# Attention and two expert layers on one core: q and k laid out by the host, another order of the first batch, a tighter conversion of the weights

## The chip, the cores and the metric

The kernel runs on one core of a Trainium2 chip. Its time is the device time of one execution in microseconds (us). The engines are TensorE (PE in the rows; PEld is its weight load), VectorE (DVE), ScalarE (ACT), GpSimd (POOL) and SyncE (SP), which here only issues DMAs. They work through their own queues in the order in which the program was written for each, and wait for one another by semaphores.

## What is computed

```python
# attention: q, k, v of 4 batches, 8 heads, 576 positions, 64 wide, float32
scores = (q @ k.T) / sqrt(64)
thresh = max(scores, axis=-1) - tau
scores = where(scores >= thresh, scores, -1e9)
attn = exp(scores - max(scores)); attn /= sum(attn) + 1e-9
x = (attn @ v)                       # as 2304 tokens x 512
# a feed-forward layer, w_in 512x2048 and w_out 2048x512, both float64
x = (relu(x @ w_in) ** 2) @ w_out
# slots: 8 experts with 4 slots each, hidden 1024
logits = x @ phi
d = softmax(logits, axis=0); c = softmax(logits, axis=1)
slots = d.T @ x
slot_out[e] = relu(slots[e] @ w1[e]) @ w2[e]      # e = 0 ... 7
out = c @ slot_out
```

## The kernel before

The work goes in pairs of heads, 16 in all, four to a batch. A pair has five query tiles: four of 128 queries of both heads from the first 512 positions (j = 0 to 3) and a mixed one (j = 4) with the last 64 queries of both heads. For each pair `prep` loads q, k and v. q and k come with positions on the partitions, and TensorE needs them with the head's width there, so `turn` transposes them by four 128x128 pieces each through the helper at L238, `evac` copies the result out of PSUM to `qt` and `kt` (L412), and `rturn`/`revac` do the same with the last 64 positions of both heads, loaded once a batch as `rem`, into a block diagonal tile `bd` whose other quarters are zero (L422).

`tiles` then makes, for each query tile: the scores (`s_mm`, L457 and L462, the mixed tile L451 and L454) into the one `s` buffer of PSUM; for each head on VectorE the scaled copy with its extreme (`top`, L478), on ScalarE the exponential (`expo`, L491), on VectorE the masked product with its sum (`keep`, L495); nine transposes of the result on TensorE and their copies on ScalarE (L534, L532). After each two tiles a group is closed: the sums' reciprocals, the product with v (L583, L572) and its scaling into `xp`, the input of the feed-forward part (L596). One unit of the feed-forward part is two query tiles of all four pairs of a batch, 256 tokens; there are eight and one for the remainders, nine in all (L867 is their first product). At most three `xp` tiles exist.

Beside the attention `conv_ops` turns the float64 weights into float32, in 32 chunks of 128x512: 16 of w_in (split into two float32r parts, L315 on ScalarE and L316 on GpSimd) and 16 of w_out (stored again by DMA, and multiplied with phi, L331). Each chunk has its load (L269, four buffers), a scale (L275), a low part (L285) and a shift (L289) on VectorE, and a sign, on GpSimd (L298) or on VectorE (L300). The first feed-forward product depends on all chunks.

The order of every queue is made when the program is written: `Plan` has each operation with an engine, a cost, what it depends on, the buffers it takes and a key. It runs a clock, and at each step gives each engine the ready operation with the smallest key. The keys are

```python
def key(p, x):
    return T0 + p * PC + x            # T0 = 20, PC = 20: a pair; TA = 4: a tile
k = C0 + n * TC                       # chunk n of the conversion: 2.604 + n * 3.458
```

to which LEAD adds a number for each kind of operation (c_scale 13.2, c_load -19.6, c_prod 65.3). Feed-forward products have keys from 100,000 on: they get TensorE when no attention is ready.

Of the kernel before, what the change touches and what calls it, by code (L numbers as in the profile page):

```python
# [9 lines left out]
F32 = mybir.dt.float32  # L10
# [4 lines left out]
AF = mybir.ActivationFunctionType  # L15
# [124 lines left out]
def tile_kernel(  # L140
# [11 lines left out]
    out: bass.AP,  # L152
):
    nc = tc.nc
    B, H, S, D = q.shape
    DM, DFF = w_in.shape
    NS = phi.shape[1]
    E, _, F = w1.shape
    NP = H // 2
# [9 lines left out]
    PAIRS = B * NP  # L169
# [3 lines left out]
    GB = 4  # L173
# [2 lines left out]
    PTB = 2  # L176
    XPB = 3
    MMB = 4
    RAWB = dict(q=1, k=1, v=2)
    WAIT = 0.0  # L180
    DQ = 2.212
    T0 = 20.0
    TA = 4.0
    PC = 20.0
    TC = 3.458
    C0 = 2.604
    LOWA = ()
    SGNP = (0, 2, 4, 6)
# [38 lines left out]
    l4 = const.tile([128, NU], F32, name="l4")  # L227
    dT = const.tile([NS, NU], F32, name="dT")
# [120 lines left out]
    def attn_ops():  # L349

        at, ac = state["at"], state["ac"]
        bd = [ac.tile([128, 2, 128], F32, name=f"bd{i}") for i in range(2)]
        vbd = [ac.tile([128, NP, 192], F32, name=f"vbd{i}") for i in range(2)]
        for t in bd + vbd:
            nc.gpsimd.memset(t, 0.0)
        ma, ps = psp["ma"], psp["s"]
        raw, rem = {}, {}
        P = [dict() for _ in range(PAIRS)]  # L360
        src = {"q": q, "k": k, "v": v}
        last = {}

        def key(p, x):
            return T0 + p * PC + x

        def prep(p):
            b, n, h0 = p // NP, p % NP, 2 * (p % NP)
            d = P[p]
            k0 = key(p - 1, 2.0) if p else 0.0  # L370
            ld = {}
            if n == 0:
                def lrem():
                    r = rem[b] = at.tile([128, NP, 2, D], F32, tag="qkrem", name="rem", bufs=1)
                    for a, nm in enumerate("qk"):
                        y = src[nm][b, :, 512:S, :].rearrange("(n h) p d -> p n h d", h=2)
                        nc.sync.dma_start(out=r[64 * a:64 * a + 64], in_=y)
# [5 lines left out]
                last["r"] = add("lrem", "SP", 1.3, lrem, [], k0 - 10, ["qkrem"], dma=0.74)  # L383
                last["v"] = add("lrem", "SP", 1.9, lvrem, [], k0 - 4, ["vbd"], dma=1.1)
            for nm in "qkv":
                def lraw(nm=nm):
                    if nm == "v":
                        t = raw[p, nm] = at.tile([128, 2, 4 * D], F32, tag=nm + "raw", name="raw", bufs=RAWB[nm])
# [10 lines left out]
            d["rem_op"], d["v_op"], d["vr_op"] = last["r"], ld["v"], last["v"]  # L399
            d["v"], d["vb"] = (lambda: raw[p, "v"]), vbd[b % 2][:, n, :]  # L400
            d["qbd"], d["kbd"] = bd[p % 2][:, 0, :], bd[p % 2][:, 1, :]

            o = {}

            def turn(nm):
                o[nm] = mm_tile()
                for j in range(4):
                    transpose(o[nm][:, j * 128:(j + 1) * 128], raw[p, nm][:, j].rearrange("p h d -> p (h d)"))

            def evac(nm):  # L410
                t = d[nm + "t"] = at.tile([128, 512], F32, tag=nm + "t", name=nm + "t", bufs=2)
                nc.scalar.activation(t, o[nm], AF.Copy)  # L412

            def rturn():
                o["r"] = mm_tile()
                transpose(o["r"][:, 0:128], rem[b][:, n].rearrange("p h d -> p (h d)"))

            def revac():
                y = o["r"][:, 0:128].rearrange("p (c s) -> p c s", c=2)
                for a in range(2):  # L420
                    i = slice(64 * a, 64 * a + 64)
                    nc.scalar.activation(bd[p % 2][i, :, i], y[i], AF.Copy)  # L422

            d["ready"] = []
            for i, nm in enumerate("kq"):
                t = add("qk_turn", "PE", 0.5, lambda nm=nm: turn(nm), [ld[nm]], k0 + 1 + i, ["mm", nm + "t"], [(nm + "raw", ld[nm])])
                e = add("qk_evac", "ACT", 0.6, lambda nm=nm: evac(nm), [t], k0 + 1 + i, [], [("mm", t)])
                d[nm + "_op"] = t
                d["ready"].append(e)
            t = add("qk_turn", "PE", 0.13, rturn, [d["rem_op"]], k0 + 3, ["mm", "bd"])  # L430
            e = add("qk_evac", "ACT", 0.55, revac, [t], k0 + 3, [], [("mm", t)])
            d["b_op"] = d["rt_op"] = t
            d["ready"].append(e)

        def tiles(p):
            d = P[p]
            b, kk = p // NP, p % NP
            G = [dict() for _ in range(3)]
            s_ops, av_ops, m_ops = [], [], []

            def tile_ops(n, j):
                k = key(p, n * TA)
                mixed = j == 4
                g = 2 if mixed else j // 2
                o, gd = {}, G[g]

                def s_mm():
                    s = ps.tile([128, 3, 512], F32, tag="s", name="s", bufs=1)
                    o["s"] = s.rearrange("p c s -> p (c s)")
                    if mixed:  # L450
                        nc.tensor.matmul(s[:, 0], d["qbd"], d["kt"], start=True, stop=True)  # L451
                        for a in range(2):
                            i = slice(64 * a, 64 * a + 64)
                            nc.tensor.matmul(s[i, 1, 0:64], d["qbd"][:, i], d["kbd"][:, i], start=True, stop=True)  # L454
# [173 lines left out]
                att.append(ev)  # L628
                av_ops.append(o)

            for n, j in enumerate(range(5)):
                tile_ops(n, j)
                if n % 2:
                    group_ops(n // 2, n)
                elif n == 4:
                    group_ops(2, n)
            for o in s_ops:
                plan.release(o, [("kt", d["k_op"]), ("qt", d["q_op"]), ("bd", d["b_op"])])
            for o in av_ops:
                plan.release(o, [("vraw", d["v_op"]), ("vbd", d["vr_op"])])  # L640
            plan.release(d["rt_op"], [("qkrem", d["rem_op"])])

        for p in range(PAIRS):
            prep(p)
            tiles(p)

    def small(shape, nm, bufs=2):
        return state["fs"].tile(shape, F32, tag=nm, name=nm, bufs=bufs)
# [523 lines left out]
```

## Time and profile before

| | |
|---|---|
| median of 3 runs | 756.98 us (754.79 to 757.75) |
| the profiled execution | 756.39 us |
| its span, first to last instruction | 754.6 us |
| TensorE busy | 691.3 us, 92% |
| VectorE busy | 422.9 us, 56% |
| ScalarE busy | 398.1 us, 53% |
| GpSimd busy | 133.8 us, 18% |
| mean granted clock of TensorE | 0.978 of full speed |

Busy times are shares of the whole span and average over stages that differ: conversion with attention, attention alone, attention with the feed-forward part, the feed-forward part alone, and the experts at the end. A matmul's listed duration includes its way through the array, and the next one starts before it ends; what one costs the engine is seen from the spacing of starts.

### The profile page before, as it was taken

What the parts mean: (1) busy time and instruction counts of PE and PEld (TensorE: products, weight loads), DVE (VectorE), ACT (ScalarE), POOL (GpSimd) and SP (SyncE); (2) the same over time, 40 slices, a digit from 0 to 9 for tenths busy, and PEclk for the clock granted to TensorE, in tenths of its full rate; (3) what the DMA queues carried; (4) which work ended last, traced back from release to release, by engine and by line L of the source; (5) the groups of instructions that cost most, each with busy time, mean ns of one, the idle gap of its engine ahead of it and who ended that gap; (6) DMA issues with size and microseconds to landing.
All of it is one profiled execution on the core that took longest, in us unless ns stands there. A gap on an engine that the chain in (4) does not pass through costs nothing.

```text
span 754.6 us, 13828 instructions
## 1 busy us (share of the span) xinstructions
PE 691.3 (92%) x5342; PEld 505.4 (67%) x5342; DVE 422.9 (56%) x1110; ACT 398.1 (53%) x790; POOL 133.8 (18%) x238
## 2 busy tenths in 40 slices
PE   1586998999999999999999999999999999998873
PEld 1253666677666686787567778767989889794311
DVE  6999888885667767625777462465133231403403
ACT  5667676777666666347667452564333343332203
POOL 5777221331121211100111100010000000000000
PEclk9978899999999999999999999999999999999998
DMA  8854545231111111010101000002920000197986
GB/s 238 229 151 150 161 140 199 86 109 43 45 27 46 36 29 45 1 43 29 29 23 23 1 1 1 29 3 90 400 84 29 1 29 2 32 357 282 388 322 251
DMA packets 70129, 78.81 MB, mean 104 GB/s; under 512 B 43952, under 2 KB 48048, under 8 KB 70064
## 3 DMA queue, kind: packets, MB, share of 16 engines
q1 hardware_dynamic: 70064, 77.94, 31.5%
q8 instruction: 42, 0.69, 0.4%
q14 instruction: 23, 0.19, 0.1%
HBM read 69.01 MB, written 8.91 MB: 103 GB/s over the span
## 4 chain that ended last, share of the span: by engine, by line
PE 79%; DVE 8%; DMA 4%; ACT 3%; issue 2%; SPq 1%; POOL 1%; POOLq 0%; DVEq 0%; ACTq 0%
PE mm L867 28%; PE mm L238 18%; PE po L583 9%; PE s L462 8%; PE mm L682 2%; PE mm L796 2%; PE po L572 2%; PE s L457 2%; DMA w<-in_moe_w_dram 2%; PE mm L998 2%; PE s L451 2%; DVE e L495 2%; DVE u L478 2%; DVE cv L289 2%; PE mm L331 1%
## 5 line engine op out<-in xcount | busy, mean ns | idle before, releaser
L867 PE MATMUL mm<-xh,w 128*128 128x256 f32 x1152 | 165.9, 287 | 0.0
L867 PEld LDWEIGHTS mm<-xh,w 128*128 128x128 f32 x1152 | 147.7, 191 | 13.7 <-issue 11.9
L495 DVE SCALAR_TENSOR_TENSOR e<-u,sm,e 128x576 f32<-128x576 f32 x144 | 120.8, 849 | 35.7 <-ACT e L491 34.0
L478 DVE TENSOR_SCALAR_CACHE_REDUCE u<-s,nscale 128x576 f32<-128x576 f32 x144 | 114.3, 811 | 44.4 <-PE s L462 39.3
L491 ACT ACTIVATE e<-u,sm 128x576 f32<-128x576 f32 x144 | 109.3, 777 | 26.0 <-DVE u L478 25.4
L534 ACT ACTIVATE pt<-mm 128x512 f32<-128x512 f32 x144 | 82.6, 596 | 56.0 <-PE mm L238 55.3
L873 ACT ACTIVATE gt<-mm 128x512 f32<-128x512 f32 x72 | 43.0, 597 | 122.8 <-PE mm L867 122.4
L238 PE MATMUL mm<-ident_r,e 128*128 128x128 f32 (+1 forms) x656 | 98.1, 285 | 9.5 <-DVE e L495 8.0
L484 POOL TENSOR_SCALAR sm<-sm,tau_p 128x1 f32<-128x1 f32 x144 | 53.6, 372 | 281.9 <-DVE u L478 218.7
L238 PEld LDWEIGHTS mm<-ident_r,e 128*128 128x128 f32 (+1 forms) x656 | 76.0, 144 | 38.2 <-issue 13.4
L867 PE MATMUL mm<-xl,w 128*128 128x256 f32 x576 | 92.4, 283 | 0.0
L867 PEld LDWEIGHTS mm<-xl,w 128*128 128x128 f32 x576 | 79.3, 192 | 0.0
L583 PE MATMUL po<-pt,raw 128*64 128x256 f32 (+1 forms) x768 | 78.3, 341 | 0.0
L462 PE MATMUL s<-kt,qt 64*128 64x512 f32 x256 | 75.1, 664 | 1.8 <-ACT kt L412 1.8
L583 PEld LDWEIGHTS po<-pt,raw 128*64 128x64 f32 x768 | 43.2, 139 | 28.6 <-issue 11.5
L879 DVE SCALAR_TENSOR_TENSOR gt<-mm,gt 128x512 f32<-128x512 f32 x18 | 12.4, 691 | 67.1 <-ACT gt L873 67.0
L238 PE MATMUL mm<-ident_r,gt 128*128 128x128 f32 x288 | 37.9, 277 | 0.1
L238 PEld LDWEIGHTS mm<-ident_r,gt 128*128 128x128 f32 x288 | 31.8, 143 | 9.2 <-issue 8.7
L881 ACT ACTIVATE gt<-gt 128x512 f32<-128x512 f32 x54 | 34.0, 630 | 1.5
L832 DVE CAST xh<-xp 128x256 fp32r<-128x256 f32 x32 | 10.5, 354 | 43.4 <-PE mm L867 43.3
L457 PE MATMUL s<-bd,qt 128*128 128x128 f32 x128 | 27.0, 293 | 7.9 <-DVE u L478 7.7
L838 POOL TENSOR_TENSOR xl<-xp,xh 128x256 fp32r<-128x256 f32 x16 | 11.6, 741 | 126.6 <-PE mm L867 126.2
(134 smaller groups left out, 828.6 us busy)
## 6 DMA issues: line engine op xcount, KB each, us to landing
w<-in_moe_w_dram SPq DMA_DIRECT2D x25, 1024.0 KB, 11.9
raw<-in_moe_w_in_dram SPq DMA_DIRECT2D x16, 512.0 KB, 4.6
raw<-in_moe_w_out_dram SPq DMA_DIRECT2D x16, 512.0 KB, 4.2
raw<-in_q_dram SPq DMA_DIRECT2D x32, 128.0 KB, 3.0
raw<-in_k_dram SPq DMA_DIRECT2D x32, 128.0 KB, 2.9
raw<-in_v_dram SPq DMA_DIRECT2D x16, 256.0 KB, 2.6
w_out<-cv SPq DMA_DIRECT2D x16, 256.0 KB, 3.7
w<-w_out SPq DMA_DIRECT2D x4, 1024.0 KB, 9.9
```

Source lines behind the costliest of these rows:

```text
L238: nc.tensor.transpose(out_, in_, ident[:n, :n])
L457: nc.tensor.matmul(s[:, 1].rearrange("p (c s) -> p c s", s=64)[:, 0:8:7], lt, d["kbd"], start=True, stop=True)
L462: nc.tensor.matmul(s[:, 2 * a], lt[i], d["kt"][i], start=True, stop=True)
L478: nc.vector.tensor_scalar(u, o["s"][:, s0:s0 + S], nscale, None, ALU.mult, ALU.min, accum_out=gd["sm"][:, c:c + 1])
L484: nc.gpsimd.tensor_scalar(sm[:, 4 + c:5 + c], sm[:, c:c + 1], tau_p, None, ALU.add)
L491: nc.scalar.activation(e, o["u", a], AF.Exp, scale=-1.0, bias=gd["sm"][:, c:c + 1])
L495: nc.vector.scalar_tensor_tensor(e, o["u", a], sm[:, 4 + c:5 + c], e, ALU.is_le, ALU.mult, accum_out=sm[:, 8 + c:9 + c])
L534: nc.scalar.activation(pt[:, 4 * x:4 * x + 4, i], o["p", x].rearrange("p (c s) -> p c s", c=4), AF.Copy)
L583: nc.tensor.matmul(po[i, :n_], lt, rh, start=m == 0, stop=m == 4)
L867: nc.tensor.matmul(o["h"][:, i * NU:(i + 1) * NU], a, c, start=n_ == 0, stop=n_ == len(terms) - 1)
L873: nc.scalar.activation(g, o["h"], AF.Relu)
L881: nc.scalar.activation(g, g, AF.Square)
```

## The change

The host hands over q and k already turned: for each batch and pair a tile of 128 rows (64 of each head) with 640 columns, 512 of the first positions in the order of the query tiles, then 128 in the block diagonal form with zeros. The kernel loads one such tile each for q and k into `qt` and `kt` (three buffers each) and multiplies from them; `turn`, `evac`, `rturn`, `revac`, `bd`, `rem` and their loads are gone. The pairs become 20 jobs: the four pairs of the first batch with query tiles 0 and 1, the same four with tiles 2 to 4, then the other twelve with all five; each job loads its own q, k and v. TC goes from 3.458 to 2.8.

```diff
-    RAWB = dict(q=1, k=1, v=2)
+    QKB = 3
-    TC = 3.458
+    TC = 2.8
-            gk=GB, l4=1, dT=1, qt=2, kt=2, bd=2, qraw=RAWB["q"], kraw=RAWB["k"], vraw=RAWB["v"], qkrem=1, vbd=2,
+            gk=GB, l4=1, dT=1, qt=QKB, kt=QKB, vraw=2, vbd=2,
...
+        jobs = [(p, js) for js in ((0, 1), (2, 3, 4)) for p in range(NP)]
+        jobs += [(p, (0, 1, 2, 3, 4)) for p in range(NP, PAIRS)]
+        P = [dict() for _ in jobs]
+        begins = [T0 + TA * sum(len(js) for _, js in jobs[:i]) for i in range(len(jobs))]
         def key(p, x):
-            return T0 + p * PC + x
+            return begins[p] + x
...
-                    t = raw[p, nm] = at.tile([128, 4, 2, D], F32, tag=nm + "raw", name="raw", bufs=RAWB[nm])
-                    for a in range(2):
-                        nc.sync.dma_start(
-                            out=t[:, :, a, :], in_=src[nm][b, h0 + a, 0:512, :].rearrange("(r j) d -> r j d", j=4)
-                        )
-                ld[nm] = add("lraw", "SP", 0.6 if nm == "v" else 1.2, lraw, [], k0 - (5 if nm != "v" else 2), [nm + "raw"], dma=0.73 if nm == "v" else 1.46)
+                    t = d[nm + "t"] = at.tile([128, SQ], F32, tag=nm + "t", name=nm + "t", bufs=QKB)
+                    nc.sync.dma_start(out=t, in_=src[nm][b, n])
+                ld[nm] = add("lraw", "SP", 0.6, lraw, [], k0 - (5 if nm != "v" else 2), [nm + ("raw" if nm == "v" else "t")],
+                             dma=0.73 if nm == "v" else 0.95)
...
-            for i, nm in enumerate("kq"):
-                t = add("qk_turn", "PE", 0.5, lambda nm=nm: turn(nm), [ld[nm]], k0 + 1 + i, ["mm", nm + "t"], [(nm + "raw", ld[nm])])
-                e = add("qk_evac", "ACT", 0.6, lambda nm=nm: evac(nm), [t], k0 + 1 + i, [], [("mm", t)])
...
-            t = add("qk_turn", "PE", 0.13, rturn, [d["rem_op"]], k0 + 3, ["mm", "bd"])
-            e = add("qk_evac", "ACT", 0.55, revac, [t], k0 + 3, [], [("mm", t)])
...
+            d["ready"] = [ld["q"], ld["k"]]
...
-                        s[:, 1].rearrange("p (c s) -> p c s", s=64)[:, 0:8:7], lt, d["kbd"], start=True, stop=True
+                        s[:, 1].rearrange("p (c s) -> p c s", s=64)[:, 0:8:7], lt, d["kt"][:, 512:SQ], start=True, stop=True
...
-                        nc.tensor.matmul(s[:, 2 * a], lt[i], d["kt"][i], start=True, stop=True)
+                        nc.tensor.matmul(s[:, 2 * a], lt[i], d["kt"][i, 0:512], start=True, stop=True)
...
-            for n, j in enumerate(range(5)):
+            for n, j in enumerate(jobs[p][1]):
...
+        if name in ("q", "k"):
+            m = a[:, :, :512].reshape(*a.shape[:2], 128, 4, -1).transpose(0, 1, 4, 3, 2).reshape(a.shape[0], -1, 128, 512)
+            r, z = a[:, :, 512:].transpose(0, 1, 3, 2), _np.zeros_like(a[:, ::2, 512:])
+            r = [_np.concatenate(x, axis=3) for x in ((r[:, ::2], z), (z, r[:, 1::2]))]
+            a = _np.concatenate([m, _np.concatenate(r, axis=2)], axis=3)
```

## Rows read from the trace of the kernel before

**Rows 1.** From the page: the span in 40 equal slices of 18.9 us. Digits are the busy share in tenths; GB/s is what the DMAs moved.

```profile
PE   1586998999999999999999999999999999998873
...
DVE  6999888885667767625777462465133231403403
...
GB/s 238 229 151 150 161 140 199 86 109 43 45 27 46 36 29 45 1 43 29 29 23 23 1 1 1 29 3 90 400 84 29 1 29 2 32 357 282 388 322 251
```

**Rows 2.** Busy time of each engine by stage: the stretch and its length in us, then busy us and count for PE, PEld, DVE, ACT and POOL, the mean granted clock of TensorE, the busy share of the DMA engines, GB/s.

```profile
0.00:83.00 83.00, 48.85 (x229) 30.17 (x229) 72.43 (x132) 53.95 (x100) 54.56 (x55) 0.86 0.65 193
83.00:157.00 74.00, 70.17 (x530) 49.22 (x526) 64.39 (x173) 54.23 (x108) 20.25 (x37) 1.00 0.45 142
157.00:180.20 23.20, 23.16 (x183) 16.70 (x182) 15.42 (x47) 16.52 (x36) 4.49 (x9) 1.00 0.21 59
180.20:686.00 505.80, 500.45 (x4051) 391.02 (x4049) 251.52 (x709) 261.06 (x525) 53.54 (x136) 1.00 0.18 60
```

**Rows 3.** The same view, of the first stretch without its first 10 us.

```profile
10.00:83.00 73.00, 48.85 (x229) 30.17 (x229) 67.53 (x120) 49.25 (x94) 49.85 (x44) 0.84 0.64 186
```

**Rows 4.** The instructions of two lines: L867, the first feed-forward product, and L275, the scale of a conversion chunk; durations in ns (least, median, most), then the first and last start in us.

```profile
L867 PE MATMUL mm<-xh,w x1152: 274/283/388, 180.2 to 675.9; 128*128 128x256 f32 x192
...
L275 ACT ACTIVATE cv<-raw x32: 647/674/714, 5.6 to 157.0; 128x512 f32<-128x512 f32 x32
```

**Rows 5.** Records of two score lines by stretch: PE busy us and count, PEld busy us and count, then the clock, the DMA share and GB/s as in rows 2. The first two rows are L457 (two records a tile), the last two L451 (two records a mixed tile).

```profile
0.00:83.00 83.00, 4.04 (x14) 2.90 (x14) 0.86 0.65 193
83.00:157.00 74.00, 5.02 (x24) 3.69 (x24) 1.00 0.45 142
...
0.00:83.00 83.00, 2.05 (x2) 0.50 (x2) 0.86 0.65 193
83.00:157.00 74.00, 3.23 (x6) 0.91 (x6) 1.00 0.45 142
```

**Rows 6.** TensorE in order of time, near 394 and 418 us: start, us, engine, line, operation, tiles, count. The rows with raw are q's and k's transposes, the one with rem is the remainders'.

```profile
393.35 0.60 PE L238 MATMUL mm<-ident_r,raw 128*128 128x128 f32 x4
393.79 0.60 PE L238 MATMUL mm<-ident_r,e 128*128 128x128 f32 x4
...
417.70 0.60 PE L238 MATMUL mm<-ident_r,raw 128*128 128x128 f32 x4
418.13 0.39 PE L457 MATMUL s<-bd,qt 128*128 128x128 f32 x2
...
419.51 0.66 PE L238 MATMUL mm<-ident_r,raw 128*128 128x128 f32 x4
420.00 0.27 PE L238 MATMUL mm<-ident_r,rem 128*128 128x128 f32 x1
```

**Rows 7.** The remainders' transposes on TensorE, one for each pair, by stretch: busy us and count (the count of the last row has one that reaches over the border).

```profile
0.00:83.00 83.00, 1.08 (x3) 0.86 0.65 193
83.00:180.20 97.20, 0.91 (x4) 1.00 0.39 122
180.20:686.00 505.80, 2.72 (x10) 1.00 0.18 60
```

**Rows 8.** TensorE in order of time from the start: its first transpose with what it waited for, and the first score matmuls.

```profile
11.65 0.66 PE L238 MATMUL mm<-ident_r,rem 128*128 128x128 f32 x2 [11.65 <-DMA rem<-in_k_dram]
...
17.02 0.77 PE L457 MATMUL s<-bd,qt 128*128 128x128 f32 x2
...
19.60 2.08 PE L462 MATMUL s<-kt,qt 64*128 64x512 f32 x4 [1.81 <-ACT kt L412]
```

**Rows 9.** VectorE's groups by line: operation, tiles, shapes, count, then busy us and the mean ns of one, and the idle time before them with what ended it.

```profile
L495 DVE SCALAR_TENSOR_TENSOR e<-u,sm,e 128x576 f32<-128x576 f32 x144 | 120.8, 849 | 35.7 <-ACT e L491 34.0 <-POOL rb L562 0.6 <-POOL sm L484 0.3
L478 DVE TENSOR_SCALAR_CACHE_REDUCE u<-s,nscale 128x576 f32<-128x576 f32 x144 | 114.3, 811 | 44.4 <-PE s L462 39.3 <-PE s L454 4.4
L289 DVE SCALAR_TENSOR_TENSOR cv<-cv,raw 128x512 int32<-128x512 int32 x32 | 30.4, 955 | 4.2 <-ACT cv L275 3.7
...
L285 DVE TENSOR_SCALAR raw<-raw 128x512 int32<-128x512 uint32 x32 | 17.7, 569 | 2.3 <-DMA raw<-in_moe_w_out_dram 1.5 <-DMA raw<-in_moe_w_in_dram 0.8
```

**Rows 10.** The conversion's two steps on VectorE with least, median and most ns, and three instructions in order of time, two of VectorE and one of GpSimd.

```profile
L285 DVE TENSOR_SCALAR raw<-raw x32: 399/422/1515, 5.6 to 147.2; 128x512 int32<-128x512 uint32 x32
...
L289 DVE SCALAR_TENSOR_TENSOR cv<-cv,raw x32: 672/688/1769, 6.3 to 158.2; 128x512 int32<-128x512 int32 x32
...
17.47 0.69 DVE L289 SCALAR_TENSOR_TENSOR cv<-cv,raw 128x512 int32<-128x512 int32 x1 [1.54 <-ACT cv L275]
...
19.27 1.47 POOL L298 TENSOR_TENSOR cv<-cv,raw 128x512 f32<-128x512 f32 x1
...
19.70 1.58 DVE L289 SCALAR_TENSOR_TENSOR cv<-cv,raw 128x512 int32<-128x512 int32 x1
```

**Rows 11.** What TensorE's transposes waited for in the first 90 us: total us, times, longest; here the one row for k's own load.

```profile
PE mm L238 <- DMA raw<-in_k_dram: 2.6, 1, 2.6
```

More of the change, by code (lines that the diff above doesn't have):

```diff
@@ L154, in tile_kernel @@
     nc = tc.nc
-    B, H, S, D = q.shape
+    B, H, S, D = v.shape
+    SQ = q.shape[3]
     DM, DFF = w_in.shape
@@ L353, in attn_ops, with prep @@
         at, ac = state["at"], state["ac"]
-        bd = [ac.tile([128, 2, 128], F32, name=f"bd{i}") for i in range(2)]
         vbd = [ac.tile([128, NP, 192], F32, name=f"vbd{i}") for i in range(2)]
-        for t in bd + vbd:
+        for t in vbd:
             nc.gpsimd.memset(t, 0.0)
         ma, ps = psp["ma"], psp["s"]
-        raw, rem = {}, {}
-        P = [dict() for _ in range(PAIRS)]
+        raw = {}
         src = {"q": q, "k": k, "v": v}
         last = {}
+        jobs = [(p, js) for js in ((0, 1), (2, 3, 4)) for p in range(NP)]
+        jobs += [(p, (0, 1, 2, 3, 4)) for p in range(NP, PAIRS)]
+        P = [dict() for _ in jobs]
+        begins = [T0 + TA * sum(len(js) for _, js in jobs[:i]) for i in range(len(jobs))]
         def key(p, x):
-            return T0 + p * PC + x
[L367 to L370, printed above, removed]
-            ld = {}
[L372 to L377, printed above, removed]
+            return begins[p] + x
+        def prep(x):
+            p, b, n, h0 = x, jobs[x][0] // NP, jobs[x][0] % NP, 2 * (jobs[x][0] % NP)
+            d = P[x]
+            k0 = key(x - 1, 2.0) if x else 0.0
+            ld = {}
+            if n == 0 and b not in last:
                 def lvrem():
@@ L382, in lvrem @@
                         nc.sync.dma_start(out=vbd[b % 2][r0:r0 + 64, :, c0:c0 + 64], in_=y[:, :, a, :])
-                last["r"] = add("lrem", "SP", 1.3, lrem, [], k0 - 10, ["qkrem"], dma=0.74)
-                last["v"] = add("lrem", "SP", 1.9, lvrem, [], k0 - 4, ["vbd"], dma=1.1)
-            for nm in "qkv":
+                last[b] = add("lrem", "SP", 1.9, lvrem, [], k0 - 4, ["vbd"], dma=1.1)
+            for nm in "kqv":
                 def lraw(nm=nm):
                     if nm == "v":
-                        t = raw[p, nm] = at.tile([128, 2, 4 * D], F32, tag=nm + "raw", name="raw", bufs=RAWB[nm])
+                        t = raw[p, nm] = at.tile([128, 2, 4 * D], F32, tag=nm + "raw", name="raw", bufs=2)
                         nc.sync.dma_start(
@@ L399, in prep @@
-            d["rem_op"], d["v_op"], d["vr_op"] = last["r"], ld["v"], last["v"]
-            d["v"], d["vb"] = (lambda: raw[p, "v"]), vbd[b % 2][:, n, :]
[L401 to L424, printed above, removed]
-            for i, nm in enumerate("kq"):
-                t = add("qk_turn", "PE", 0.5, lambda nm=nm: turn(nm), [ld[nm]], k0 + 1 + i, ["mm", nm + "t"], [(nm + "raw", ld[nm])])
-                e = add("qk_evac", "ACT", 0.6, lambda nm=nm: evac(nm), [t], k0 + 1 + i, [], [("mm", t)])
-                d[nm + "_op"] = t
-                d["ready"].append(e)
@@ L435, in tiles @@
+            d["v_op"], d["vr_op"], d["q_op"], d["k_op"] = ld["v"], last[b], ld["q"], ld["k"]
+            d["v"], d["vb"] = (lambda: raw[p, "v"]), vbd[b % 2][:, n, :]
+            d["ready"] = [ld["q"], ld["k"]]
         def tiles(p):
             d = P[p]
-            b, kk = p // NP, p % NP
+            b, kk = jobs[p][0] // NP, jobs[p][0] % NP
             G = [dict() for _ in range(3)]
@@ L450, in s_mm @@
                     if mixed:
-                        nc.tensor.matmul(s[:, 0], d["qbd"], d["kt"], start=True, stop=True)
+                        nc.tensor.matmul(s[:, 0], d["qt"][:, 512:SQ], d["kt"][:, 0:512], start=True, stop=True)
                         for a in range(2):
                             i = slice(64 * a, 64 * a + 64)
-                            nc.tensor.matmul(s[i, 1, 0:64], d["qbd"][:, i], d["kbd"][:, i], start=True, stop=True)
+                            nc.tensor.matmul(s[i, 1, 0:64], d["qt"][:, 512 + 64 * a:576 + 64 * a], d["kt"][:, 512 + 64 * a:576 + 64 * a], start=True, stop=True)
                         return
@@ L629, in group_ops @@
                 av_ops.append(o)
-            for n, j in enumerate(range(5)):
+            for n, j in enumerate(jobs[p][1]):
                 tile_ops(n, j)
-                if n % 2:
-                    group_ops(n // 2, n)
-                elif n == 4:
+                if j % 2:
+                    group_ops(j // 2, n)
+                elif j == 4:
                     group_ops(2, n)
             for o in s_ops:
-                plan.release(o, [("kt", d["k_op"]), ("qt", d["q_op"]), ("bd", d["b_op"])])
+                plan.release(o, [("kt", d["k_op"]), ("qt", d["q_op"])])
             for o in av_ops:
                 plan.release(o, [("vraw", d["v_op"]), ("vbd", d["vr_op"])])
[L641 to L645, printed above, removed]
+        for x in range(len(jobs)):
+            prep(x)
+            tiles(x)
     def small(shape, nm, bufs=2):
@@ L1158 @@
     for name in _INS:
-        a = _np.ascontiguousarray(inputs[name])
+        a = inputs[name]
+        if name in ("q", "k"):
[3 more added lines that the diff above has]
+            a = _np.concatenate([m, _np.concatenate(r, axis=2)], axis=3)
+        a = _np.ascontiguousarray(a)
         if name == "tau":
```

2 lines of the change are left out of this document (removed).

## The prediction

> **What bounds the kernel now.** I read four views, in this order. First the page's forty slices [rows 1]: TensorE's line goes 1, 5, 8, 6 and then stays at 9 or 8 to the tail, while VectorE's is at 9 in slices 2 to 4 and falls to 2 to 6 later. So two stretches have two different limits. Then the busy time by stage [rows 2]: from 83 to 157 us TensorE is busy 70.17 of 74 us and VectorE 64.39; from 157 to 180.2 TensorE 23.16 of 23.2; from 180.2 to 686, the feed-forward stretch, 500.45 of 505.8, with VectorE at half. Behind 83 us TensorE is the limit, and whatever leaves its queue there shortens the kernel by that much. Before 83 us it is not: TensorE is busy 48.85 us, at a mean granted clock of 0.86, VectorE 72.43. Third, what VectorE lacks there: from 10 us on it is busy 67.53 of 73 us [rows 3], so 5.5 us are idle; 5.1 more lie in the first 10 us, before the first weights have landed. VectorE sets the pace of the first 83 us, with the conversion of the weights beside the attention. Fourth, the order: the first feed-forward matmul starts at 180.2 us and the last chunk of the conversion enters ScalarE at 157.0 [rows 4]. By 157 us the score matmuls of 23 query tiles have started (38 records of L457 at two a tile, 8 of L451 at two a tile) [rows 5]; a pair of heads has five tiles, so that is 4.6 pairs of 16.
>
> **The change part by part. The turning of q and k.** Each pair loses eight transposes of q and k, one of the remainders, two 128x512 copies out of PSUM and two small ones on ScalarE. What a transpose costs TensorE is the spacing of starts, not its listed duration: four take 0.43 us (417.70 to 418.13) or 0.44 (393.35 to 393.79), and the ninth starts 0.49 us after the four before it and is followed at once [rows 6]. I take 0.43 + 0.44 + 0.11 = 0.98 us a pair, 15.7 us for 16 pairs. The remainder's transposes show which pair lies where: three before 83 us, four from there to 180.2, the other nine behind [rows 7]. The nine lie where TensorE alone is the limit: 9 x 0.98 = -8.8 us, in full. The four lie where TensorE is ahead of VectorE by only 70.17 - 64.39 = 5.8 us, and the denser conversion puts more on VectorE there for each tile: I credit half, -2.0 us (bounds -3.9 and 0). The three before 83 us lie under VectorE's work, but their eight transposes also run at the lower clock and sit ahead of scores that VectorE waits for: half, -1.5 us (bounds -2.9 and 0). The copies on ScalarE are credited with nothing: it is busy 53.95 of 83 us, so its own time is covered by VectorE's.
>
> **The start.** Now TensorE gets its first operand at 11.65 us, when the remainders land, and the first long score matmul starts at 19.60 [rows 8]; scores, transposes and copies hang on three DMAs and two evictions. Afterwards two DMAs of 320 KB stand between, issued behind the same four weight loads. That lets the first scores start some 8 to 10 us earlier, but VectorE has conversion to do meanwhile; only its idle time can be filled. Of the 5.5 us I take -2.0 (bounds -5.5 and 0).
>
> **The conversion.** TC is the distance of priorities between 32 chunks, and a smaller one lets a chunk pass ahead of attention. The last chunk's scale had key 2.604 + 31 x 3.458 + 13.2 = 123.0 and gets 102.6; a tile is worth 4.0, so some 5.1 tiles fewer are ahead of it. A tile costs VectorE twice 0.811 + 0.849 us [rows 9], 3.3 us, so the conversion ends and the feed-forward part starts about 17 us earlier, near 163 us. That by itself is worth nothing: TensorE is full from 83 us on with attention, and the attention that is passed over has to be done later on the same engine. It would only fill gaps: 3.8 us between 83 and 157. I take 0 (bounds -3.8 and 0). With it move its loads, 512 KB each on SP's queue, past those of q, k and v, and the 16 stores; SP blocks on the four buffers anyway, so the loads can't run further ahead than four chunks.
>
> The price of bunching is contention. A chunk's two VectorE steps take 0.399 and 0.672 us at best but up to 1.515 and 1.769, and the long ones lie beside GpSimd's work on the same weights: at 17.47 us L289 takes 0.69, and at 19.70 it takes 1.58, with GpSimd's L298 running from 19.27 [rows 10]. The means are 0.569 and 0.955 [rows 9], so over 32 chunks the excess is now 32 x (0.170 + 0.283) = 14.5 us. If all 16 chunks of w_in had both at the worst, it would be 16 x (1.116 + 1.097) = 35.4 us: 20.9 more. GpSimd's instructions stay the same in number and it is busy 54.56 of the first 83 us already; most collisions that can be had are there. I take +2.0 (bounds 0 and +20.9).
>
> The Trainium skill (SBUF — State Buffer, Who interferes with whom) speaks against this part: a VectorE instruction with two SBUF inputs and a GpSimd instruction that reads SBUF exclude each other for a whole instruction. The trace agrees in kind, by the 1.58 us above, of an instruction with two such inputs. By that rule every further meeting costs a whole GpSimd instruction, and the sum would go to the dearer end.
>
> **The order of the first batch.** Tiles 0 and 1 of four pairs come first, then tiles 2 to 4; the feed-forward part's first unit is complete after 8 tiles and not after 17. With the conversion done at about tile 18, neither order makes it wait: 0. The price is that q, k and v of the first batch are loaded twice, 20 sets of 0.9 MB for 16 of 0.77. In the first 83 us that is some 3 MB more, and one to three chunks of weights, on top of 83 us x 193 GB/s = 16 MB [rows 2]: about 245 GB/s, where the page shows slices at 388 and 400 [rows 1]. The cover is this room; q and k now move in rows of 2560 bytes instead of 256. Without it, a late load would show as TensorE's wait for k did, 2.6 us once [rows 11], for each of the first eight sets at most: bounds 0 and +20.8, taken 0, since the loads run one set ahead.
>
> The sum: -8.8 - 2.0 - 1.5 - 2.0 + 2.0 = -12.3 us against the profiled execution's 756.39 (span 754.6 and 1.8 around it): 744.1. The median of the runs is 756.98, 0.6 above the profiled one, so I stay at 744.
>
> **The rivals.** (a) The gain before the feed-forward part is eaten: the denser conversion makes VectorE the limit up to 160 us, all seven early pairs give nothing, and contention rises by 4 us: 756.4 - 8.8 + 4 = 751.6. For it: VectorE's 64.39 of 74 us. Against it: TensorE is still the fuller one there.
> (b) It goes better: all 16 pairs count, VectorE's 5.5 us of idle are filled, and TensorE's 3.8 us of gaps too: 756.4 - 15.7 - 5.5 - 3.8 = 731.4. For it: the scores are ready much earlier at the start. Against it: VectorE has still the same work to do first.
> (c) Slower, by the collisions of VectorE and GpSimd in the first 60 us: at the full 20.9 us the sum is 756.4 - 14.3 + 20.9 = 763.0. It decides from 14.3 us of extra excess on, when 29 of the possible 35.4 us are reached. For it: the long instructions in the trace. Against it: GpSimd's work is no larger, and only its overlap could grow. The rule of the Trainium skill named above is this rival's.
> (d) No difference: the double loads come late in the crowded start, and four or five sets at 2.6 us, 10 to 13 us, cancel the gain: 754 to 757. For it: DMA moves 230 to 240 GB/s in the first two slices already. Against it: larger rows.
>
> **How the numbers follow.** Chances: the forecast 0.58, (a) 0.13, (b) 0.13, (c) 0.06, (d) 0.08, and 0.02 for something not named. About 0.5%, 3.8 us, is what a measurement of this kernel can tell from no change. Faster by that (under 753.2): the forecast, (b) and nearly all of (a), 0.83. Within it: (d) and the rest of (a), 0.09. Slower: (c) and the unnamed, 0.08. The range goes from 732, next to (b), to 753, beyond (a); what is left out is (c), (d) and the far end of (b), under 0.2.
>
> **What would show it.** In the changed kernel's profile L238 has no group from raw or rem; the first long score matmul starts near 10 us; the last conversion scale is near 140 and the first feed-forward matmul near 163 us, with about 18 to 19 tiles' scores begun by the first of these. From there to the tail TensorE is as full as before, and the stretch of the feed-forward part is longer by the attention left over, less 0.98 us a pair. VectorE's two conversion steps have means near 0.6 and 1.0 us. The prediction is wrong if those means go far above that (rival c), if TensorE waits for kt or qt by DMA in the first 60 us (rival d), or if TensorE shows gaps behind 100 us, which the sum doesn't hold: a feed-forward unit waiting for attention that was put off, or scores waiting for VectorE.

## The result, and the profile after

| | before | changed |
|---|---|---|
| median | 755.88 us (4 runs, 753.65 to 757.75) | 738.16 us (4 runs, 737.51 to 741.05) |
| ratio, 95% interval | | 0.9769 (0.9747 to 0.9792) |
| profiled execution | 756.39 us, span 754.6 | 741.05 us, span 739.2 |
| mean granted clock | 0.978 | 0.974 |

The change takes off 17.7 us, 2.3%; 12.3 were forecast, and 738.2 lies inside the range of 732 to 753. The profiled execution of the changed kernel is the slowest of its four, 2.9 us above the median, so its span shows 15.4 us less and not 17.7. In its lines L830 is the first feed-forward product (L867 before), L421, L426 and L415 the scores (L457, L462, L451), L276, L286, L290 and L301 the conversion's scale, low part, shift and sign (L275, L285, L289, L300).

Busy time by stage of the changed kernel, columns as in [rows 2]; the third row ends where the first feed-forward product starts, and the fourth runs from there to the last of them:

```profile
0.00:10.00 10.00, 0.00 (x0) 0.00 (x0) 4.54 (x12) 4.51 (x6) 3.92 (x10) 1.00 0.73 244
10.00:83.00 73.00, 49.45 (x237) 29.15 (x238) 71.13 (x131) 50.03 (x90) 51.27 (x49) 0.86 0.68 221
83.00:159.00 76.00, 71.06 (x518) 49.92 (x515) 62.02 (x171) 48.84 (x97) 20.65 (x32) 0.93 0.54 171
159.00:661.20 502.20, 497.39 (x4001) 386.84 (x3999) 261.54 (x733) 253.76 (x501) 55.91 (x145) 1.00 0.16 55
```

From 10 to 83 us VectorE lacks 1.9 us instead of 5.5 [rows 3]. The stretch before the first feed-forward product is 21.2 us shorter than before, and the one behind it is 6.0 us longer. In the kernel before it ran from 180.2 to 676.4:

```profile
180.20:676.40 496.20, 491.24 (x3961) 384.95 (x3959) 246.19 (x693) 257.04 (x515) 52.68 (x136) 1.00 0.17 54
```

The order in time of the same two lines as in [rows 4]:

```profile
L830 PE MATMUL mm<-xh,w x1152: 274/283/388, 159.0 to 660.7; 128*128 128x256 f32 x192
...
L276 ACT ACTIVATE cv<-raw x32: 647/674/712, 5.8 to 133.6; 128x512 f32<-128x512 f32 x32
```

TensorE from the start, as in [rows 8], and the longest of three later waits, which the profile names only "issue", with VectorE's instruction just before its end:

```profile
11.87 0.77 PE L421 MATMUL s<-kt,qt 128*128 128x128 f32 x2 [11.87 <-DMA qt<-in_q_dram]
12.57 2.08 PE L426 MATMUL s<-kt,qt 64*128 64x512 f32 x4
...
45.46 0.81 DVE L442 TENSOR_SCALAR_CACHE_REDUCE u<-s,nscale 128x576 f32<-128x576 f32 x1
...
46.38 0.77 PE L421 MATMUL s<-kt,qt 128*128 128x128 f32 x2 [4.43 <-issue]
```

The first long score matmul starts at 12.57 us and not at 19.60. The wait for q at 11.87 is the only one that the profile puts down to q or k in the whole execution. The three waits of "issue", 10.2 us in all, I read as waits for VectorE: the one shown ends 0.1 us after VectorE's second reading of the one `s` buffer (45.46 + 0.81 = 46.27), and this pair's loads of k and q had been issued at 27.6 and 28.1 us, where none takes more than 8.0 to land.

### The profile page after: what moved, and what is told of

Read it like the earlier page. It is cut to its first block, busy times and chain, and to the rows that moved or that the text cites. A ratio compares the mean times of both kernels' runs of the same rounds, so it can differ in the third digit from the quotient of the medians.

```text
span 739.2 us, 13383 instructions
## 1 busy us (share of the span) xinstructions
PE 674.4 (91%) x5198; PEld 489.8 (66%) x5198; DVE 423.7 (57%) x1110; ACT 373.4 (51%) x726; POOL 133.6 (18%) x236
## 4 chain that ended last, share of the span: by engine, by line
PE 79%; DVE 8%; DMA 4%; ACT 4%; issue 2%; POOL 1%; SPq 1%; DVEq 0%; ACTq 0%; POOLq 0%
PE mm L830 29%; PE mm L239 16%; PE po L547 9%; PE s L426 8%; PE mm L759 2%; PE mm L645 2%; PE po L536 2%; DMA w<-in_moe_w_dram 2%; PE mm L961 2%; PE s L421 2%; DVE raw L286 1%; PE s L415 1%; DVE cv L290 1%; DVE e L459 1%; PE mm L332 1%
## 5 line engine op out<-in xcount | busy, mean ns | idle before, releaser
L830 PE MATMUL mm<-xh,w 128*128 128x256 f32 x1152 | 166.4, 287 | 0.0
L830 PEld LDWEIGHTS mm<-xh,w 128*128 128x128 f32 x1152 | 147.6, 191 | 13.7 <-issue 11.0
L459 DVE SCALAR_TENSOR_TENSOR e<-u,sm,e 128x576 f32<-128x576 f32 x144 | 122.7, 862 | 35.0 <-ACT e L455 32.9
L830 PE MATMUL mm<-xl,w 128*128 128x256 f32 x576 | 92.5, 283 | 0.0
L830 PEld LDWEIGHTS mm<-xl,w 128*128 128x128 f32 x576 | 79.3, 192 | 0.0
L426 PE MATMUL s<-kt,qt 64*128 64x512 f32 x256 | 77.0, 680 | 0.0
L421 PE MATMUL s<-kt,qt 128*128 128x128 f32 x128 | 27.3, 297 | 29.4 <-DMA qt<-in_q_dram 11.9
L421 PEld LDWEIGHTS s<-kt,qt 128*128 128x128 f32 x128 | 20.7, 201 | 33.7 <-issue 19.8
L801 POOL TENSOR_TENSOR xl<-xp,xh 128x256 fp32r<-128x256 f32 x16 | 12.3, 780 | 115.9 <-PE mm L830 82.6
```

Of the source, the lines that this page charges most:

```text
L421: nc.tensor.matmul(s[:, 1].rearrange("p (c s) -> p c s", s=64)[:, 0:8:7], lt, d["kt"][:, 512:SQ], start=True, stop=True)
L426: nc.tensor.matmul(s[:, 2 * a], lt[i], d["kt"][i, 0:512], start=True, stop=True)
L459: nc.vector.scalar_tensor_tensor(e, o["u", a], sm[:, 4 + c:5 + c], e, ALU.is_le, ALU.mult, accum_out=sm[:, 8 + c:9 + c])
L830: nc.tensor.matmul(o["h"][:, i * NU:(i + 1) * NU], a, c, start=n_ == 0, stop=n_ == len(terms) - 1)
```

## The experiments

All ratios are against the kernel before, run on the same chip, with their 95% intervals. The first four take the change apart, the next four put work back or push TC further, the last four ask where the gain before the feed-forward part is from.

**The layout alone.**

```diff
-        jobs = [(p, js) for js in ((0, 1), (2, 3, 4)) for p in range(NP)]
-        jobs += [(p, (0, 1, 2, 3, 4)) for p in range(NP, PAIRS)]
+        jobs = [(p, (0, 1, 2, 3, 4)) for p in range(PAIRS)]
-    TC = 2.8
+    TC = 3.458
```

> The host's layout of q and k alone: the order of the first batch and TC stay as they were. Theory (the transposes are what is gained, 0.98 us a pair, in full behind 157 us and in part before): 756 - 14 = 742 us, with the first feed-forward product still near 177 us. Rival (denser conversion and the new order carry a good part of the 17.7 us, by an earlier feed-forward part): 747 us or more.

Measured: 737.67 us, ratio 0.9764 (0.9742 to 0.9787), the same as the whole change. Its stages, around the first feed-forward product at 169.7 us:

```profile
10.00:83.00 73.00, 51.18 (x240) 27.74 (x240) 69.87 (x131) 48.84 (x89) 51.58 (x46) 0.86 0.58 191
83.00:169.70 86.70, 84.02 (x630) 57.63 (x630) 75.64 (x211) 60.47 (x119) 27.42 (x45) 1.00 0.43 141
169.70:657.50 487.80, 482.50 (x3885) 377.08 (x3883) 247.22 (x693) 243.66 (x480) 52.15 (x136) 1.00 0.16 55
```

At 169.7 us this kernel has begun 27 tiles (44 score records at two a tile, 10 of the mixed kind at two), the same 27 as the kernel before at 180.2. So the two can be laid side by side: 10.5 us are gained before the feed-forward part and 496.2 - 487.8 = 8.4 us in it. The rival falls: neither TC nor the order is needed for the gain. My theory missed too, on the good side: 742 us and a first feed-forward product near 177 were expected. The 10.5 us can be divided by TensorE's own rows. Up to the first feed-forward product it is busy 48.85 + 70.17 + 23.16 = 142.2 us in the kernel before [rows 2] and 51.18 + 84.02 = 135.2 here, 7.0 us less, about the seven pairs' turns (6.9); it is idle 38.0 and 34.5 us, 3.5 less. The clocks are close, 0.84 and 0.86 from 10 to 83 us and 1.00 behind.

**The layout and the order.** TC = 3.458 in the changed kernel.

> The layout and the new order of the first batch, with TC = 3.458. Theory (the order is worth nothing, since the conversion ends later than the first unit in either order): the same as the layout alone within 2 us, near 742. Rival (the order lets TensorE go over to the feed-forward part sooner): nearer to the changed kernel's 738 than to the layout alone.

Measured: 742.10 us, 0.9806 (0.9782 to 0.9829). Slower than the layout alone by 0.0042 of 756, 3.2 us, though the intervals overlap; my theory had 2 at most. The rival can't be told from it, because the layout alone came out at the changed kernel's time.

**The layout and TC.** The old order of the jobs in the changed kernel.

> The layout and TC = 2.8, the pairs in their old order, each loaded once. Theory: the order is worth nothing, so this is the changed kernel's time within 2 us, 738, with the first feed-forward product near 159 us. Rival: without the order the first unit is complete too late for the earlier end of the conversion, and 742 or more comes out.

Measured: 741.89 us, 0.9810 (0.9791 to 0.9829), 3.5 us above the layout alone, with the first feed-forward product at 158.8 as foreseen. The theory, 738 within 2, falls. The rival's 742 is nearly met, but not for its reason: the feed-forward part starts as early as in the changed kernel (159.0), and the two profiled executions have the same span, 739.2 us. VectorE's conversion steps of this kernel by line, columns as in [rows 9]:

```profile
L290 DVE SCALAR_TENSOR_TENSOR cv<-cv,raw 128x512 int32<-128x512 int32 x32 | 26.5, 832 | 3.3 <-ACT cv L276 2.2 <-issue 0.8
L286 DVE TENSOR_SCALAR raw<-raw 128x512 int32<-128x512 uint32 x32 | 23.0, 735 | 1.2 <-DMA raw<-in_moe_w_in_dram 1.2
L301 DVE SCALAR_TENSOR_TENSOR cv<-raw,cv 128x512 int32<-128x512 int32 x16 | 16.6, 1039 | 0.1
```

and of the layout alone:

```profile
L290 DVE SCALAR_TENSOR_TENSOR cv<-cv,raw 128x512 int32<-128x512 int32 x32 | 27.2, 852 | 2.3 <-ACT cv L276 0.9 <-issue 0.8
L286 DVE TENSOR_SCALAR raw<-raw 128x512 int32<-128x512 uint32 x32 | 18.5, 603 | 1.8 <-DMA raw<-in_moe_w_in_dram 1.2 <-DMA raw<-in_moe_w_out_dram 0.6
L301 DVE SCALAR_TENSOR_TENSOR cv<-raw,cv 128x512 int32<-128x512 int32 x16 | 13.5, 847 | 0.1
```

The sums are 66.1 and 59.2 us, 6.9 us more of VectorE's time for the same instructions. That the denser conversion does it is not shown: with the same TC the sum is 59.6 in the next run and 60.0 in the changed kernel. I read it as the work of one order of the queues; it isn't seen in the span.

**TC alone, in the kernel before.**

> The kernel before with TC = 2.8 and nothing else. Theory (TensorE is full from 83 us on, so an earlier feed-forward part only reorders its work; contention may cost 2 us): 754 to 758 us, no difference. Rival (the earlier end of the conversion is worth something by itself): 752 us or less.

Measured: 754.79 us, 0.9975 (0.9959 to 0.9992), 1.9 us less. The feed-forward part starts at 158.2 instead of 180.2, 22 us earlier, and 1.9 us come out of it. That an earlier start reorders the work of a full TensorE, and saves next to nothing, is borne out here most plainly. VectorE's conversion steps cost the same as in the kernel before, 59.6 us and 59.4. First the sign of the kernel before, beside [rows 9], then the three of this run:

```profile
L300 DVE SCALAR_TENSOR_TENSOR cv<-raw,cv 128x512 int32<-128x512 int32 x16 | 11.3, 704 | 0.2
...
L289 DVE SCALAR_TENSOR_TENSOR cv<-cv,raw 128x512 int32<-128x512 int32 x32 | 28.1, 882 | 4.1 <-ACT cv L275 3.3
...
L285 DVE TENSOR_SCALAR raw<-raw 128x512 int32<-128x512 uint32 x32 | 18.5, 598 | 0.8 <-DMA raw<-in_moe_w_in_dram 0.7 <-DMA raw<-in_moe_w_out_dram 0.2
L300 DVE SCALAR_TENSOR_TENSOR cv<-raw,cv 128x512 int32<-128x512 int32 x16 | 13.0, 812 | 0.2
```

**Nine transposes put back for each of the last nine jobs.**

```diff
             d["ready"] = [ld["q"], ld["k"]]
+            if x >= 11:
+                def again():
+                    t = mm_tile()
+                    for i in range(9):
+                        j = i % 4
+                        transpose(t[:, j * 128:(j + 1) * 128], d["kt"][:, j * 128:(j + 1) * 128])
+                t = add("again", "PE", 1.13, again, [ld["k"], ld["q"]], k0 + 2, ["mm"])
+                plan.release(t, [("mm", t), ("kt", ld["k"])])
```

> The changed kernel with nine transposes of 128x128 put back on TensorE for each of its last nine jobs, from the tile kt into PSUM; nobody reads or waits for the result. It measures the price of a pair's turns alone in the stretch where TensorE is the limit. Theory: 9 x 0.98 = 8.8 us more than the changed kernel, 747 us. Rival (the gaps between matmuls take them in): under 743 us.

Measured: 749.41 us, 0.9899 (0.9878 to 0.9919), 0.0130 of 756 or 9.8 us above the changed kernel. The stage says it more exactly than the medians do:

```profile
160.00:671.00 511.00, 507.43 (x4082) 395.12 (x4081) 261.00 (x733) 255.94 (x501) 58.51 (x145) 1.00 0.16 54
```

It has 81 records more than the changed kernel's stage (4082 against 4001) and is 511.0 - 502.2 = 8.8 us longer: 0.109 us for a transpose, 0.98 for nine, the number read from the spacing of starts.

**The same for the first nine jobs.** The condition is `x < 9`.

> The same nine transposes for each of the first nine jobs instead, which are all scored before the first feed-forward product. Theory (VectorE sets the pace in the first 83 us, and TensorE only behind): 3 to 5 us more than the changed kernel, 741 to 743 us. Rival (TensorE counts everywhere): 8.8 us more, 747. Rival (VectorE is the limit up to 159 us): no difference, 738 to 739.

Measured: 742.39 us, 0.9816 (0.9784 to 0.9848), 3.6 us above the changed kernel. The stage behind the first feed-forward product is as long as the changed kernel's, 502.0 us, and it starts at 162.3 instead of 159.0, with the same 23 tiles begun: 3.3 of the 8.8 us are seen. All that lies before it:

```profile
0.00:162.30 162.30, 130.06 (x832) 90.79 (x832) 138.03 (x313) 104.12 (x192) 77.27 (x90) 0.92 0.60 194
```

TensorE is busy 9.5 us more than in the changed kernel (49.45 + 71.06 = 120.5) and idle 6.2 us less (32.2 against 38.5): in this start its waits take in more than half of the turns, as I had said. The six executions run from 739.55 to 746.68 us and the interval overlaps that of the changed kernel, so the time alone would not show it.

**TC = 2.2 and TC = 1.6 in the changed kernel.**

> The changed kernel with TC = 2.2: the last scale has the key 84.0, so some 4.7 tiles fewer lie before the end of the conversion, and the feed-forward part begins near 145 us. Theory (that only reorders TensorE's work): 738 us within 2. Rival (an earlier start of the feed-forward part gives time by itself): 735 or less. Second rival (denser conversion collides on VectorE and GpSimd): 741 or more.

> The changed kernel with TC = 1.6, last key 65.4, near the 11th tile: the feed-forward part begins near 130 us. Theory: still 738 within 3. Rival (gain by the earlier start): under 733. Second rival (collisions, and attention that comes late for the feed-forward part): 742 or more.

Measured: 744.79 us, 0.9852 (0.9833 to 0.9871), and 748.64 us, 0.9896 (0.9880 to 0.9912). They are 6.3 and 9.6 us above the changed kernel; the theory of 738 within 2 or 3 falls, and so does the rival of a gain. The stages from 10 to 83 us, first of 2.2, then of 1.6:

```profile
10.00:83.00 73.00, 44.00 (x201) 26.00 (x201) 69.66 (x121) 47.44 (x86) 52.36 (x44) 0.88 0.71 229
```

```profile
10.00:83.00 73.00, 42.23 (x195) 25.92 (x195) 70.17 (x116) 45.28 (x81) 53.10 (x42) 0.91 0.73 239
```

VectorE is nearly as full as in the changed kernel (71.13), but TensorE has run 201 and 195 records there instead of 237. The conversion that goes ahead gives TensorE nothing to do in these 73 us, and the attention that is put off is missing from them. The feed-forward part starts at 156.9 and 140.9 us, but what was put off makes the stage behind it 507.3 and 527.2 us long, with TensorE full: the idle time of the start is never won back. Up to the first feed-forward product TensorE is idle 45.3 and 45.1 us, against 38.5 in the changed kernel. The second rival, collisions, stands beside this. The three conversion steps take 64.5 and 63.4 us against 60.0, and the masked product (L459, before L495) 122.9 and 124.7 against 122.7, together 4.7 and 5.4 us more of VectorE's time in stretches where it is nearly full. How much of the 6.3 and 9.6 us comes from that is not shown.

**The layout alone, with the transposes of the first seven pairs put back.** The addition is that of the runs above, with `x < 7`.

> The host's layout alone (TC = 3.458, old order), with nine transposes put back on TensorE for each of the first seven pairs, off the chain: nobody waits for them. With the layout alone the first feed-forward product came 10.5 us earlier than before, at the same tile, where the prediction had 5.5. Theory now (TensorE's own time counts for nearly all seven pairs in this schedule): 6 to 7 us more than the layout alone, 744, and the first feed-forward product near 176 us. Rival (VectorE's pace hides much of it, and the gain came from the shorter chain before the scores): 2 to 3.5 us more, 740 to 741.

Measured: 747.94 us, 0.9893 (0.9864 to 0.9922), 9.8 us above the layout alone for 6.9 us of transposes. This is more than either theory had. The first feed-forward product starts at 191.3, not at 176, behind more attention: the stage behind it is 10.5 us shorter than with the layout alone. The written order of the queues came out another one, with 29 tiles begun instead of 27. TensorE's waits at the scores for VectorE to read `s` are not the reason: 15.4 us here, 15.1 in the layout alone. Its clock is lower:

```profile
83.00:191.30 108.30, 101.53 (x718) 69.58 (x715) 83.84 (x230) 66.83 (x130) 26.91 (x48) 0.94 0.38 123
```

The layout alone has 1.00 there up to its first feed-forward product, and the mean clocks of the six executions lie between 0.965 and 0.971, where five of the layout alone have 0.971 to 0.982. By the row the lower clock is worth up to 0.06 x 108.3 = 6.5 us, an estimate; so the 9.8 us are not the price of the turns alone.

**The same with ScalarE's copies and the chain.**

```diff
+                def copy():
+                    y, s_ = d["kt"], o["t"]
+                    d["kt"] = z = at.tile([128, SQ], F32, tag="kz", name="kz", bufs=2)
+                    nc.scalar.activation(s_, d["qt"][:, 0:512], AF.Copy)
+                    nc.scalar.activation(s_[:, 0:128], d["qt"][:, 512:SQ], AF.Copy)
+                    nc.scalar.activation(z[:, 0:512], y[:, 0:512], AF.Copy)
+                    nc.scalar.activation(z[:, 512:SQ], y[:, 512:SQ], AF.Copy)
+                u = add("copy", "ACT", 1.8, copy, [t], k0 + 1, ["kz"], [("mm", t), ("kt", ld["k"])])
+                d["kz_op"], d["ready"] = u, [u]
```

The buffers of `qt` and `kt` go from three to two here.

> As the run before, and ScalarE's four copies a pair are put back too, behind the transposes; the scores of the first seven pairs read k from the copy, so the chain load, transposes, copies, scores is there again. What differs from the kernel before in these pairs is then only the loads. If the chain is what was gained: 8 to 11 us more than the layout alone, 746 to 749. If TensorE's time is all: the same as the run before within 1.5 us. If ScalarE's copies matter little and the loads did it: both near 738 to 740.

Measured: 743.70 us, 0.9835 (0.9806 to 0.9865), 5.4 us above the layout alone, and below the run with the transposes alone. None of the three expectations has this number. The chain is there in the trace, and the first long score starts at 19.30 us, nearly as late as in the kernel before (19.60):

```profile
11.02 2.15 PE L239 MATMUL mm<-ident_r,kt 128*128 128x128 f32 x9 [11.02 <-DMA kt<-in_k_dram]
18.57 0.80 PE L439 MATMUL s<-kz,qt 128*128 128x128 f32 x2 [5.39 <-ACT kz L412]
19.30 2.08 PE L444 MATMUL s<-kz,qt 64*128 64x512 f32 x4
```

Yet this run isn't the slower of the two, so the chain is not what was gained. Its stages up to the first feed-forward product:

```profile
10.00:83.00 73.00, 52.45 (x267) 31.54 (x267) 66.63 (x133) 53.12 (x102) 48.17 (x47) 0.88 0.57 185
83.00:177.10 94.10, 89.01 (x672) 61.83 (x671) 76.92 (x209) 66.57 (x134) 26.22 (x43) 1.00 0.41 134
```

At 177.1 us it has begun 27 tiles (44 and 10 score records), as the layout alone has at 169.7 and the kernel before at 180.2, and its mean clocks (0.976 to 0.982) are those of the layout alone. So the three can be laid side by side. It is 7.4 us behind the layout alone: TensorE is busy 141.5 us against 135.2, 6.3 more, and idle 35.6 against 34.5, 1.1 more. Most of what seven pairs' turns cost in this schedule is TensorE's own time. The 3.1 us by which it stays ahead of the kernel before go with what it doesn't put back, such as the loads of q and k as they were; no run tests that apart.

**The layout alone with TC = 4.2.**

> The layout alone with a sparser conversion, TC = 4.2: the last scale has the key 146.0, some 5.7 tiles later. TC = 2.2 and 1.6 were slower by 6 and 10 us than 2.8. Theory (denser conversion leaves TensorE with less attention under VectorE's work; sparser gives more): 734 to 738 us. Rival (3.458 was the best place, since sparser conversion meets the full xp buffers before the feed-forward part can start): 739 to 745.

Measured: 739.78 us, 0.9788 (0.9754 to 0.9822). Not told apart from 3.458, and outside the theory's 734 to 738: a sparser conversion does not go on gaining. The rival's time is met, its reason (full `xp` buffers) not looked at.

**Order and TC in the kernel before**, q and k turned on the chip.

> The kernel before with the new order of the first batch and TC = 2.8, q and k turned on the chip as before. Theory (neither gives time by itself): 754 to 759 us. Rival (order and TC together are worth the 3 us by which the changed kernel is ahead of either alone with the layout): 752 or less.

Measured: 768.48 us, 1.0158 (1.0122 to 1.0193), 12 us slower, which neither theory had. With turning on the chip the new order turns the first batch twice, four pairs more, some 3.9 us. The rest I can't settle. Its stages in the profiled execution show TensorE at a granted clock of 0.90 between 83 and 170.2 us, and 7.1 us of gaps behind:

```profile
83.00:170.20 87.20, 83.02 (x593) 62.17 (x592) 64.39 (x176) 59.68 (x119) 23.66 (x36) 0.90 0.48 142
170.20:689.50 519.30, 512.25 (x4102) 397.40 (x4100) 263.12 (x739) 271.69 (x545) 57.78 (x147) 1.00 0.16 53
```

In the kernel before, those values are 1.00 and 5.0 us (491.24 of 496.2 busy). The clock is not the whole of it: two executions with a mean of 0.981, inside the 0.974 to 0.985 of the kernel before, still take 766.0 and 765.9 us. So order and TC cost much with q and k turned on the chip and next to nothing with the host's layout.

## Why the prediction was right, and where not

**The nine late pairs, -8.8 us: right to a few tenths.** 8.4 us between the kernel before and the layout alone at the same tile, 8.8 us in the run that puts nine jobs' transposes back. Had the listed duration been taken (128 transposes of 296 ns and 16 of 307), a pair would have come to 2.7 us, nearly three times as much; the spacing of starts is the price.

**The seven early pairs and the start, -2.0 - 1.5 - 2.0 = -5.5 us: mis-sized.** The layout alone gains 10.5 us before the feed-forward part. This is the term that failed: I credited TensorE's turns with half, 3.5 us, because VectorE is busy beside them [rows 2], and they count nearly in full. TensorE's busy time up to the same tile falls by 7.0 us in the layout alone, and 6.3 come back with the turns. VectorE is the fuller engine in the first 83 us and the emptier one behind, and being the fuller did not make it hide the other's work. The start, credited with 2.0 for VectorE's idle time, lies in the 3.5 us by which TensorE's own idle time falls. With the first long score put back to 19.30 us, 1.1 of them come back; what the other 2.4 are stays open. In the other schedule, that of the changed kernel, only 3.3 of 8.8 us of turns are seen, near the half that I assumed, and no run takes its start apart further. So the 744 proves little of its terms: the early pairs were put too low and the conversion too dear, both to the same side, and the sum stayed 5.4 us short of the 17.7 inside a range that was 21 us wide.

**The conversion, 0 and +2.0 us: right in kind.** That an earlier feed-forward part is worth next to nothing by itself is shown by TC alone (22 us earlier, 1.9 us gained); with 2.2 and 1.6 it starts earlier still and the time is longer. With the layout, TC costs 3.5 us and the order 3.2, each without the other, and both together 0.4 (0.9769 against 0.9764, within either interval). I forecast +2.0 for both; the whole is nearer 0. VectorE's conversion steps and the masked product in the changed kernel, columns as in [rows 9]:

```profile
L459 DVE SCALAR_TENSOR_TENSOR e<-u,sm,e 128x576 f32<-128x576 f32 x144 | 122.7, 862 | 35.0 <-ACT e L455 32.9 <-POOL sm L448 1.2 <-ACT pt L498 0.2
L290 DVE SCALAR_TENSOR_TENSOR cv<-cv,raw 128x512 int32<-128x512 int32 x32 | 24.6, 777 | 3.6 <-ACT cv L276 2.4 <-issue 0.8
L286 DVE TENSOR_SCALAR raw<-raw 128x512 int32<-128x512 uint32 x32 | 21.9, 702 | 1.1 <-DMA raw<-in_moe_w_in_dram 1.1
L301 DVE SCALAR_TENSOR_TENSOR cv<-raw,cv 128x512 int32<-128x512 int32 x16 | 13.5, 844 | 0.1
```

The conversion's sum is 60.0 us; before it was 30.4 + 17.7 [rows 9] and 11.3 for the sign, 59.4. Rival (c) fell: the two steps that it counted take 46.5 us against 48.1, and 49.5 at the most, in the run with the layout and TC; the rival needed 14 us more than before. My bound left out two steps that also have two inputs in SBUF, the sign (13.5 us against 11.3) and the masked product (122.7 against 120.8).

The mechanism itself is there. In the changed kernel a VectorE step with two such inputs starts while GpSimd works:

```profile
32.45 1.59 POOL L317 TENSOR_TENSOR w<-cv,w 128x512 fp32r<-128x512 f32 x1 [1.19 <-ACT w L316]
...
32.86 1.74 DVE L290 SCALAR_TENSOR_TENSOR cv<-cv,raw 128x512 int32<-128x512 int32 x1
```

It takes 1.07 us more than at best (0.672), and 1.18 us of GpSimd's instruction were left when it started. By the rule that the prediction named (the Trainium skill, SBUF — State Buffer, Who interferes with whom), whichever of the two starts first decides which one waits; the trace agrees here. So a meeting costs what is left of the earlier instruction, and not always a whole one as I had it. How many meetings a schedule makes is what decides, and that is read from a trace.

**The loads, 0: right.** Rival (d) fell. The loads of 320 KB land in 3.1 us (k) and 4.0 (q) at the median, and apart from the first operand the profile shows no wait of TensorE for one, though the DMA moves 221 GB/s from 10 to 83 us where it was 186 [rows 3].

**The marks.** The first feed-forward product was put near 163 us (159.0), the last conversion scale near 140 (133.6), 18 to 19 tiles begun by then (17), the first long score near 10 (12.57, 7.0 us earlier than before and not 8 to 10), the means of VectorE's two conversion steps near 0.6 and 1.0 us (0.702 and 0.777). TensorE's gaps in the feed-forward stretch stay as they were, 4.8 us in 502.2 against 5.0 in 496.2. At 159.0 us 23 tiles have begun, against 27 at 180.2 before; the four that are put off go with the longer stage behind: 502.2 - 487.8 = 14.4 us against the layout alone, 3.6 us a tile. Rival (a) fell with the early pairs, and (b), at 731.4, is about as far from the 738.2 measured as the forecast: what it held of the early pairs is nearly so in the layout alone, what it held of TensorE's gaps is not, with 4.9 us idle of 76 from 83 to 159 us.

## What to carry to other kernels

Price work on a pipelined engine by the spacing of starts, then ask for each stage whether that engine is the one that the stage waits for: there the price counts in full, and here it did to a few tenths. Where two engines are both nearly full and wait for each other tile by tile, the fuller one need not hide the other's work: half a credit was too little in one schedule here and about right in another, and the written order of the queues moved the result by several microseconds. Before reading a few microseconds, look whether the clock was the same. When a change has three parts, run the parts: the layout alone gave the whole gain, and the two that went with it added nothing that could be measured.

## What the runs showed of the hardware

TensorE's granted clock differs from one kernel to the next in the first 180 us, and its mean from one execution to the next. In the changed kernel's profiled execution it falls once more (it was 0.66 to 0.95 between 20 and 70 us) to the lower of its two levels (1.2 against 2.4 GHz) around 90 us, behind a stretch in which TensorE twice waited, 0.43 and 1.49 us:

```profile
87.27 0.66 PE L239 MATMUL mm<-ident_r,cv 128*128 128x128 f32 x4 [0.43 <-POOL cv L299]
89.41 1.10 PE L415 MATMUL s<-kt,qt 128*128 128x512 f32 x2 [1.49 <-DVE u L442]
90.44 0.48 PE L418 MATMUL s<-kt,qt 128*64 128x64 f32 x4
90.85 1.12 PE L239 MATMUL mm<-ident_r,e 128*128 128x128 f32 x4
91.76 1.75 PE L332 MATMUL mm<-l,wt 128*128 128x32 f32 x8
...
100.91 0.66 PE L239 MATMUL mm<-ident_r,e 128*128 128x128 f32 x4
```

Four transposes take 0.91 us there (90.85 to 91.76) and 0.43 or 0.44 at the full clock [rows 6]; and the stretch from 90 to 100 us shows TensorE busy throughout at 0.52:

```profile
90.00:100.00 10.00, 10.00 (x43) 7.14 (x43) 6.72 (x21) 5.71 (x11) 3.31 (x5) 0.52 0.59 198
```

Of the five executions of the layout alone the slowest, 741.97 us, has a mean granted clock of 0.971 and the fastest, 736.82, has 0.982. By the row above, such a dip is worth up to 10.0 x (1 - 0.52) = 4.8 us, an estimate. Differences of 3 us between kernels of this family lie within it, and I read the 3 us that TC and the order cost with that in mind.
